# Nine chunks of attention ahead of the first MLP, two token blocks side by side from its first step

## The chip, the cores and the metric

One core of one Trainium2 chip runs the whole program. The metric is the device time of one execution in microseconds (us). The engines are TensorE (PE in the profile, its weight loads PEld), VectorE (DVE), ScalarE (ACT) and GpSimd (POOL); all DMAs are issued from SyncE's queue (SP).

## The reference

Three stages follow one another in float32. Attention runs over B=4 batches, H=8 heads, S=768 steps, head size 48; the two MLPs run over the 3072 tokens of 384 features that attention gives.

```python
for t in range(S):
    state = alpha[:, :, t, :, None] * state + einsum('bhd,bhe->bhde', k[:, :, t], v[:, :, t])
    y[:, :, t] = einsum('bhd,bhde->bhe', q[:, :, t], state)
x = y as (3072 tokens, 384)
h = x @ w_in                      # 384 -> 2048
x = (h * sigmoid(h)) @ w_out      # 2048 -> 384
out = (sigmoid(x @ w_gate) * (x @ w_val)) @ w_out2   # 384 -> 1536 -> 384
```

The weights arrive as 64-bit floats and are turned into float32 on the chip.

## The kernel before, in words

**Attention** is cut into 24 chunks c of 128 tokens, six to a batch. For a chunk, `prep(c, step)` (L262) makes cumulative products of alpha by two scans on DVE: G backward (L277) and A forward (L287). The keys are multiplied by G (L285), the queries by A (L290), and AE (L283) is the decay of the state over the chunk. `scores(c)` (L296) transposes the keys (tile T) and multiplies keys with queries into two PSUM banks (tile S, L310). `scores_done(c)` masks S into M on DVE (L323), copies T to KT on ACT (L326) and squares G and A for a range check on ACT (L260). `results(c)` multiplies the state W with the queries (L338), adds M times the values (L345) and multiplies KT with the values (L355): this last product, U, is what the chunk adds to the state. U lies in the first bank of the chunk's own S. `state(c)` adds U to W on DVE (L363, a copy at L365 for the first chunk of a batch) and multiplies W by AE of the next chunk (L367, one instruction of 112x448). The last chunk of a batch has no T and no U, the first no L338. `y_out(c)` copies the result on ACT (L382) and moves it by six small DMAs (L385, L387) into tile xf; `x_out(c)` splits xf into a rounded part xh on ACT (L394) and a rest xl (L396). The products at L283, L285, L290, L367 and L396 run on POOL for chunks up to ALONE=8, later on DVE.

**The first MLP** runs over items (b, f): block b of 512 tokens (four chunks, six blocks), slice f of 128 of the 2048 features. `mm_in` is nine matmuls of 128x512 into a bank of `ps_h` (two banks, tag h), `act` applies Silu (L568) and splits the result into gh (ACT, L576) and gl (DVE, L577), and `mm_out` is nine matmuls (L549 to L551) that add to the block's three output banks. `mm_out` of an item follows two items later. Block 0 holds the banks of group 0, the other blocks those of group 1; `x2_out` empties them after the last slice.

**Weights** are converted by `Way`. A pair j holds one or two weight tiles (pairs 0 to 2 hold one, then w_in's slice j-1 and w_out's slice j-2, 18 pairs). `bit()` does one sixth of a pair: bits 0 to 2 are L459, L461 and L463 on DVE (with L451 on ACT in bit 0), bit 3 is L482 and L486 on ACT, the load of the pair after next and L494 on DVE, bit 4 is L496 and L497 on DVE, bit 5 is L504 on POOL. `half(True)`, `half(False)` do half a pair with the same operations, two pairs interleaved; raw and temporary tiles are used again two pairs later.

**The order** is written by hand; each engine runs its instructions in that order. The front loop (L690 to L702) runs over the LEAD=5 first chunks: scores of c+1, `states()` (that is `state(c-1)`), `prep` of c+2 with `scores_done(c+1)` between its steps, `x_out(c-1)`, results of c, `y_out(c)`, then CONV[c] bits, 21 in all. Then follow seven items of block 0 alone (LAG=7) with two halves each, in which chunks 5 to 8 are done; then nine times an item of block 0 and one of block 1 with one half each; then the rest of block 1, with chunks 9 to 11 at (1, 10) to (1, 14); then blocks 2 to 5, each with four chunks. SCORES and RESULTS say at which item, and at which place in it (0 behind `mm_in`, 1 behind `mm_out`), a chunk's steps stand; `prep` lies three and two items ahead of the scores.

The second MLP has the same form with two products in; its weights are converted in the last block of the first and in its own first steps.

Of the kernel before, what the change touches and what calls it, by code (L numbers as in the profile page):

```python
# [7 lines left out]
F32 = mybir.dt.float32  # L8
# [5 lines left out]
AF = mybir.ActivationFunctionType  # L14
# [3 lines left out]
P = 128  # L18
# [3 lines left out]
C = 128  # L22
# [11 lines left out]
BLOCKS = [(N * i, N) for i in range(NT // N)]  # L34
NB = len(BLOCKS)

LEAD = 5
LAG = 7

ALONE = 8  # L40
WARM = 3

BITS = 6
SINGLE = 3
CONV = {1: 5, 2: 5, 3: 6, 4: 5}

SCORES = {6: (0, 1, 0), 7: (0, 3, 0), 8: (0, 5, 0), 9: (1, 10, 0), 10: (1, 11, 1), 11: (1, 13, 0)}
RESULTS = {5: (0, 0, 0), 6: (0, 2, 0), 7: (0, 4, 0), 8: (0, 6, 0), 9: (1, 11, 0), 10: (1, 12, 1), 11: (1, 14, 0)}
for _c in range(12, NC):
    SCORES[_c] = (_c // 4 - 1, (0, 4, 8, 11)[_c % 4], 0)  # L50
    RESULTS[_c] = (_c // 4 - 1, (2, 6, 10, 13)[_c % 4], 0)

# [125 lines left out]
def gated_attention_then_mlps(ctx: ExitStack, tc: tile.TileContext, qka, a0, v, w_in, w_out, w_gate, w_val, w_out2, out):  # L178
# [83 lines left out]
    def prep(c, step, p0=0, p1=NP, mul=None):  # L262


        mul = mul or (nc.gpsimd if c <= ALONE else nc.vector)
        t = qk[c]
        lo, hi = p0 * C, p1 * C
        if step == 0:
            if p0 == 0:
                Gt[c] = ap.tile([DP, NP * C], F32, tag="G", name="G", bufs=2)  # L270
                At[c] = ap.tile([DP, NP * C], F32, tag="A", name="A", bufs=2)
            g = Gt[c]
            nc.vector.memset(g[:, hi - 1 : hi], 1.0)
            a_next = t[:, A_OFF + hi - 1 : A_OFF + lo : -1]
            d_g = dg[:, NP * C - 2 :: -1] if lo == 0 and hi == NP * C else dg[:, hi - 2 : lo - 1 : -1] if lo else dg[:, hi - 2 :: -1]
            g_r = g[:, hi - 2 : lo - 1 : -1] if lo else g[:, hi - 2 :: -1]
            nc.vector.tensor_tensor_scan(g_r, a_next, d_g, 1.0, op0=ALU.mult, op1=ALU.add)  # L277
            whole = ap.tile([DP, NP], F32, tag="whole", name="whole")
            nc.vector.tensor_scalar(whole[:, p0:p1], g[:, lo:hi:C], LEAST, None, op0=ALU.max)
            nc.vector.reciprocal(d1[:, lo:hi:C], whole[:, p0:p1])  # L280
            if c % CB:
                AE[c] = ap.tile([DP, NP], F32, tag="aend", name="aend", bufs=2)
                mul.tensor_tensor(AE[c], a0s[:, c, :], g[:, 0::C], op=ALU.mult)  # L283
            k = t[:, NP * C + lo : NP * C + hi]
            mul.tensor_tensor(k, k, g[:, lo:hi], op=ALU.mult)  # L285
        elif step == 1:
            nc.vector.tensor_tensor_scan(At[c][:, lo:hi], t[:, A_OFF + lo : A_OFF + hi], d1[:, lo:hi], 0.0, op0=ALU.mult, op1=ALU.add)  # L287
        else:
            q = t[:, lo:hi]
            mul.tensor_tensor(q, q, At[c][:, lo:hi], op=ALU.mult)  # L290
# [39 lines left out]
    def results(c, g):  # L330


        y = Y[c] = bank(g)
        first = c % CB == 0
        if not first:
            for p in range(NP):

                nc.tensor.matmul(  # L338
                    y[:DP, p * C : (p + 1) * C], W[:, p], qk[c][:, p * C : (p + 1) * C], start=p == 0, stop=False, skip_group_check=True
                )  # L340
        for p in range(NP):
            m = M[c, p // 2]
            for j in range(2):
                r = 64 * j
                nc.tensor.matmul(  # L345
                    y[r : r + D, p * C : (p + 1) * C], vt[c][:, 2 * p + j], m[:, j, p % 2], start=first and p == 0, stop=True, skip_group_check=True
                )
        s = S.pop(c)
        if not last_of(c):
            U[c] = s[:DP, 0, : NP * DP].rearrange("r (p d) -> r p d", p=NP)  # L350
            kt = KT.pop(c)
            for p in range(NP):
                for j in range(2):
                    r = 64 * j
                    nc.tensor.matmul(U[c][r : r + D, p, r : r + D], kt[:, p, r : r + D], vt[c][:, 2 * p + j], start=True, stop=True)  # L355

    def state(c):

        u = U.pop(c)
        for r in (0, 64):  # L360
            s, x = W[r : r + D, :, r : r + D], u[r : r + D, :, r : r + D]
            if c % CB:
                nc.vector.tensor_tensor(s, x, s, op=ALU.add)  # L363
            else:
                nc.vector.tensor_copy(s, x)  # L365
        mul = nc.gpsimd if c <= ALONE else nc.vector
        mul.tensor_tensor(W, W, AE[c + 1].rearrange("r (p d) -> r p d", d=1).to_broadcast([DP, NP, DP]), op=ALU.mult)  # L367

    def block_of(c):
        for b, (t0, n) in enumerate(BLOCKS):  # L370
# [18 lines left out]
    def x_out(c):  # L389
        b, o = block_of(c)  # L390
        if o == 0:
            xh[b], xl[b] = (X(i, F32R) for i in x_at[b])
        x = xf.pop(c)
        nc.scalar.activation(xh[b][:, :, o : o + C], x, AF.Copy, accum_out=chk[:, c, 2:3])  # L394
        mul = nc.gpsimd if c <= ALONE else nc.vector
        mul.tensor_tensor(xl[b][:, :, o : o + C], x, xh[b].bitcast(F32)[:, :, o : o + C], op=ALU.subtract)  # L396


# [240 lines left out]
    with tc.manual_schedule():  # L639
# [28 lines left out]
        def states():  # L668
            while late and (last_of(late[0]) or late[0] + 1 in AE):
                c = late.pop(0)  # L670
                if not last_of(c):
                    state(c)

        def results_done(c):
            late.append(c)
            if c >= LEAD:
                states()
            y_out(c)
            if c + 4 < NC:
                load_chunk(c + 4)  # L680
                load_values(c + 4)
# [6 lines left out]
            prep(1, s)  # L688
        scores_done(0)
        for c in range(LEAD):  # L690
            scores(c + 1, (c + 1) % 2, True)
            states()
            prep(c + 2, 0)
            scores_done(c + 1)
            prep(c + 2, 1)
            prep(c + 2, 2)
            if c:
                x_out(c - 1)
            results(c, c % 2)
            results_done(c)  # L700
            for _ in range(CONV.get(c, 0)):
                way1.bit()  # L702
        states()
        way1.n_half = 2 * SINGLE

        def steps(items):

            at = {x: i for i, x in enumerate(items)}
            todo = {}

            def put(i, place, what, c):
                todo.setdefault((i, place), []).append((what, c))

            for c, (b, f, end) in SCORES.items():
                put(at[b, f], end, "scores", c)
                if c > LEAD + 1:
                    put(at[b, f] - 3 if c != ALONE + 1 else at[0, LAG - 2], 2, "prep0", c)
                    put(at[b, f] - 2, 2, "prep1", c)
            for c, (b, f, end) in RESULTS.items():
                put(at[b, f], end, "results", c)  # L720
                put(at[b, f] + 1 if c != ALONE else at[1, NF1 - LAG - 1], 1, "x_out", c)
            put(0, 1, "x_out", LEAD - 1)
            return todo

        items = [(0, f) for f in range(LAG)]
        for f in range(LAG, NF1):
            items += [(0, f), (1, f - LAG)]
        items += [(1, f) for f in range(NF1 - LAG, NF1)] + [(b, f) for b in range(2, NB) for f in range(NF1)]
        todo = steps(items)

        def tensor(i, place):
            for what, c in todo.get((i, place), ()):
                g = int(c <= ALONE)
                if what == "scores":
                    scores(c, g, False)
                elif what == "results":
                    results(c, g)

        def others(i, place):
            for what, c in todo.get((i, place), ()):  # L740
# [13 lines left out]
        for i, (b, f) in enumerate(items):  # L754
            if (b, f) == (NB - 1, 0):
                at_stack.close()
                bp["b"] = main.enter_context(tc.tile_pool(name="bp", bufs=3))
                bp["x"] = main.enter_context(tc.tile_pool(name="bx", bufs=NX))
                way2.load(0)
                way2.n_half = -2  # L760
            h = mm_in(ps_h, "h", "in", b, f)
            tensor(i, 0)
            way = way1 if i < 2 * NF1 - LAG else way2 if b == NB - 1 else None
            act(b, f, h, None, "out", way)
            others(i, 0)
            others(i, 2)
            if len(pend) > 2:
                mm_out()
            tensor(i, 1)
            others(i, 1)  # L770
            if i < LAG:
                way1.half(True)
                way1.half(False)
            if (b, f) == (NB - 1, NF1 - 4):
                x2_split(0)
            if (b, f) == (NB - 1, NF1 - 1):
                x2_split(1)
# [66 lines left out]
```

## Time and profile before

| | us |
|---|---|
| median of 3 runs (1008.43 to 1008.48) | 1008.44 |
| profiled execution | 1007.8 |
| its span, first to last instruction | 1006.1 |
| PE busy | 957.5 (95%) |
| DVE busy | 521.8 (52%) |
| ACT busy | 385.7 (38%) |
| POOL busy | 127.1 (13%) |

The span is cut into stages by what PE does: the front loop to about 59 us, block 0 alone and the catching up to about 140 us, and from there to 997 us a PE that hardly waits. A busy DVE includes time in which one of its instructions stands blocked, so durations of one kind of instruction are compared with the shortest of that kind.

### The profile page before, as it was taken

Reading aid. Unit: us, or ns where it says so; the run is one execution under the profiler, and the core shown is the slowest. Engines: PE = TensorE matmul, PEld = TensorE weight load, DVE = VectorE, ACT = ScalarE, POOL = GpSimd, SP = SyncE. Lnnn points to the kernel's source line nnn. Section 1 sums busy time; section 2 is a strip of 40 time slices with the busy share of each in tenths; the row PEclk is TensorE's granted clock in tenths of the full one; section 3 lists DMA queues with packets and bytes.
Section 4 is the critical chain, followed back from the end, with each engine's and each line's share of the span. In section 5 each row is a group of like instructions: output and inputs, shape, how many; then the busy total and the mean of one; then the engine's idle time right before and its main releaser. Section 6 shows DMA issues by size and latency. Waiting matters only on the chain.

```text
span 1006.1 us, 12880 instructions
## 1 busy us (share of the span) xinstructions
PE 957.5 (95%) x5008; PEld 786.3 (78%) x5008; DVE 521.8 (52%) x782; ACT 385.7 (38%) x713; POOL 127.1 (13%) x117
## 2 busy tenths in 40 slices
PE   6577899999999999999999999999999999999996
PEld 4465678877888888888888888888888888888885
DVE  8999888464554454453589755663222222222221
ACT  3344566444433433443457443343222222221221
POOL 4554433200000000000033122220000000000000
PEclk8778899999999999999999999999999999999999
DMA  7665352012112112000322111100100000000001
GB/s 184 174 164 160 107 165 83 0 45 87 44 51 80 44 44 78 18 8 13 130 95 94 63 64 64 63 0 1 63 1 1 32 1 0 32 1 1 32 1 35
DMA packets 40038, 58.38 MB, mean 58 GB/s; under 512 B 5216, under 2 KB 28928, under 8 KB 39968
## 3 DMA queue, kind: packets, MB, share of 16 engines
q1 hardware_dynamic: 39968, 57.47, 19.4%
q8 instruction: 41, 0.67, 0.3%
q14 instruction: 29, 0.24, 0.1%
HBM read 48.02 MB, written 4.72 MB: 52 GB/s over the span
## 4 chain that ended last, share of the span: by engine, by line
PE 85%; DVE 9%; issue 2%; POOL 1%; ACT 1%; DMA 1%; SPq 0%; DVEq 0%; POOLq 0%; ACTq 0%
PE h L549 12%; PE h L551 12%; PE h L550 12%; PE s L549 8%; PE s L551 7%; PE s L550 7%; PE y L551 4%; PE y L549 4%; PE y L550 4%; PE v L549 3%; PE v L551 3%; PE v L550 3%; PE s L310 2%; PE y L345 2%; PE y L338 2%
## 5 line engine op out<-in xcount | busy, mean ns | idle before, releaser
L549 PE MATMUL h<-x,w 128*128 128x512 f32 x582 | 228.5, 393 | 4.1 <-ACT w L486 2.3
L551 PE MATMUL h<-x,w 128*128 128x512 f32 x582 | 227.7, 391 | 1.5 <-POOL w L504 1.5
L577 DVE TENSOR_TENSOR gl<-g,gh 128x512 fp32r<-128x512 f32 x168 | 130.0, 774 | 190.8 <-ACT gh L576 190.8
L550 PE MATMUL h<-x,w 128*128 128x512 f32 x582 | 227.5, 391 | 0.0
L576 ACT ACTIVATE gh<-g 128x512 fp32r<-128x512 f32 x168 | 106.2, 632 | 157.9 <-DVE g L571 154.9
L549 PE MATMUL s<-gl,w 128*128 128x512 f32 x336 | 135.8, 404 | 1.5 <-DVE gl L577 1.5
L549 PEld LDWEIGHTS h<-x,w 128*128 128x128 f32 x582 | 109.8, 189 | 29.6 <-ACT w L486 3.5
L550 PE MATMUL s<-gh,w 128*128 128x512 f32 x336 | 132.0, 393 | 0.0
L551 PE MATMUL s<-gh,w 128*128 128x512 f32 x336 | 132.0, 393 | 0.0
L551 PEld LDWEIGHTS h<-x,w 128*128 128x128 f32 x582 | 109.6, 188 | 26.0 <-POOL w L504 2.8
L568 ACT ACTIVATE g<-h 128x512 f32<-128x512 f32 x96 | 57.2, 596 | 184.2 <-PE h L551 184.2
L550 PEld LDWEIGHTS h<-x,w 128*128 128x128 f32 x582 | 109.6, 188 | 23.0
L571 DVE TENSOR_TENSOR g<-v,g 128x512 f32<-128x512 f32 x46 | 31.8, 692 | 178.7 <-PE v L551 178.7
L504 POOL TENSOR_TENSOR w<-tmp,w 128x384 fp32r<-128x384 f32 x36 | 44.3, 1251 | 443.7 <-ACT w L486 443.7
L570 ACT ACTIVATE g<-h 128x512 f32<-128x512 f32 x72 | 43.1, 599 | 144.4 <-PE h L551 144.4
L549 PEld LDWEIGHTS s<-gl,w 128*128 128x128 f32 x336 | 63.5, 189 | 17.5 <-DVE gl L577 1.9
L551 PEld LDWEIGHTS s<-gh,w 128*128 128x128 f32 x336 | 63.7, 189 | 13.8
L550 PEld LDWEIGHTS s<-gh,w 128*128 128x128 f32 x336 | 63.7, 190 | 12.3
L550 PE MATMUL y<-gh,w 128*128 128x512 f32 x168 | 66.0, 393 | 0.0
L549 PE MATMUL y<-gl,w 128*128 128x512 f32 x168 | 65.9, 393 | 0.0
L551 PE MATMUL y<-gh,w 128*128 128x512 f32 x168 | 65.8, 391 | 0.0
L551 PE MATMUL v<-x,w 128*128 128x512 f32 x138 | 53.8, 390 | 0.0
(114 smaller groups left out, 1170.9 us busy)
## 6 DMA issues: line engine op xcount, KB each, us to landing
x<-in_moe_w_out SPq DMA_DIRECT2D x16, 384.0 KB, 4.4
x<-in_qka SPq DMA_DIRECT2D x12, 448.0 KB, 4.3
qk<-in_qka SPq DMA_DIRECT2D x11, 448.0 KB, 4.3
v<-in_v SPq DMA_DIRECT2D x24, 192.0 KB, 4.2
x<-in_moe_w_in SPq DMA_DIRECT2D x16, 288.0 KB, 3.7
raw<-in_moe_w_gate SPq DMA_DIRECT2D x12, 384.0 KB, 3.6
raw<-in_moe_w_val SPq DMA_DIRECT2D x12, 384.0 KB, 3.9
raw<-in_moe_w_out SPq DMA_DIRECT2D x12, 384.0 KB, 3.8
```

The source lines that it names most:

```text
L310: nc.tensor.matmul(S[c][:, j, p * C : (p + 1) * C], t[r : r + D, NP * C + p * C : NP * C + (p + 1) * C], t[r : r + D, p * C : (p + 1) * C] ...
L338: nc.tensor.matmul(y[:DP, p * C : (p + 1) * C], W[:, p], qk[c][:, p * C : (p + 1) * C], start=p == 0, stop=False, skip_group_check=True)
L345: nc.tensor.matmul(y[r : r + D, p * C : (p + 1) * C], vt[c][:, 2 * p + j], m[:, j, p % 2], start=first and p == 0, stop=True, skip_group_c ...
L504: nc.gpsimd.tensor_tensor(l, b[:, i * SW : (i + 1) * SW].bitcast(F32), h.bitcast(F32), op=ALU.subtract)
L549: nc.tensor.matmul(ps, wh, x_l, start=first, stop=False)
L550: nc.tensor.matmul(ps, wh, x_h, start=False, stop=False)
L551: nc.tensor.matmul(ps, wl, x_h, start=False, stop=last)
L568: nc.scalar.activation(g, h, AF.Silu)
L570: nc.scalar.activation(g, h, AF.Sigmoid)
L571: nc.vector.tensor_tensor(g, val, g, op=ALU.mult)
L576: nc.scalar.activation(gh, g, AF.Copy)
L577: nc.vector.tensor_tensor(gl, g, gh.bitcast(F32), op=ALU.subtract)
```

## The change

LEAD becomes 9: the front loop does chunks 0 to 8, and `prep` of c+2 stands as a whole ahead of `scores_done(c+1)`, with `states()` of chunk 8 right behind its results. CONV spreads the same 21 bits as three to each of the chunks 2 to 8. From the first item on, blocks 0 and 1 alternate; at the six slices in SKIP block 0 goes ahead alone, so that it ends at item 25 of 0 to 31. Each of the first 28 items has one half of a pair, the five in MORE a second one. Chunks 9, 10 and 11 stand at (1, 12) to (1, 15), and one more `mm_out` is done ahead of block 2. In the front loop U is put into a bank of `ps_h` and no longer into S. The keys' product (L285) and AE (L283) go from POOL to DVE for chunks 1 to 8, and the decay of W (L367) goes from one POOL instruction to four ACT instructions of 112x112, each with a scale per partition, for states 0 to 7, and to DVE for state 8.

```diff
-LEAD = 5
-LAG = 7
-ALONE = 8
+LEAD = 9
+SKIP = (3, 6, 9, 12, 14, 15)
-CONV = {1: 5, 2: 5, 3: 6, 4: 5}
-SCORES = {6: (0, 1, 0), 7: (0, 3, 0), 8: (0, 5, 0), 9: (1, 10, 0), 10: (1, 11, 1), 11: (1, 13, 0)}
-RESULTS = {5: (0, 0, 0), 6: (0, 2, 0), 7: (0, 4, 0), 8: (0, 6, 0), 9: (1, 11, 0), 10: (1, 12, 1), 11: (1, 14, 0)}
+CONV = {2: 3, 3: 3, 4: 3, 5: 3, 6: 3, 7: 3, 8: 3}
+MORE = (4, 8, 12, 16, 20)
+SCORES = {9: (1, 12, 0), 10: (1, 13, 1), 11: (1, 14, 1), 12: (2, 0, 0)}
+RESULTS = {9: (1, 13, 0), 10: (1, 14, 0), 11: (1, 15, 0), 12: (2, 2, 0)}
+X_OUT = {8: (1, 11), 11: (1, 15)}
+DECAYS = {10: ((1, 9), (1, 10)), 11: ((1, 13), (1, 13)), 12: ((1, 14), (1, 15))}
...
     def prep(c, step, p0=0, p1=NP, mul=None):
-        mul = mul or (nc.gpsimd if c <= ALONE else nc.vector)
+        mul = mul or (nc.gpsimd if c < LEAD else nc.vector)
...
-                mul.tensor_tensor(AE[c], a0s[:, c, :], g[:, 0::C], op=ALU.mult)
+                nc.vector.tensor_tensor(AE[c], a0s[:, c, :], g[:, 0::C], op=ALU.mult)
             k = t[:, NP * C + lo : NP * C + hi]
-            mul.tensor_tensor(k, k, g[:, lo:hi], op=ALU.mult)
+            nc.vector.tensor_tensor(k, k, g[:, lo:hi], op=ALU.mult)
...
-            U[c] = s[:DP, 0, : NP * DP].rearrange("r (p d) -> r p d", p=NP)
+            u = ps_h.tile([P, N], F32, tag="h", name="u")[:DP] if c < LEAD else s[:DP, 0]
+            U[c] = u[:, : NP * DP].rearrange("r (p d) -> r p d", p=NP)
...
-        mul = nc.gpsimd if c <= ALONE else nc.vector
-        mul.tensor_tensor(W, W, AE[c + 1].rearrange("r (p d) -> r p d", d=1).to_broadcast([DP, NP, DP]), op=ALU.mult)
+        if c < LEAD - 1:
+            for p in range(NP):
+                nc.scalar.activation(W[:, p], W[:, p], AF.Copy, scale=AE[c + 1][:, p : p + 1])
+        else:
+            nc.vector.tensor_tensor(W, W, AE[c + 1].rearrange("r (p d) -> r p d", d=1).to_broadcast([DP, NP, DP]), op=ALU.mult)
...
         for c in range(LEAD):
-            scores(c + 1, (c + 1) % 2, True)
+            if c + 1 < LEAD:
+                scores(c + 1, (c + 1) % 2, True)
             states()
-            prep(c + 2, 0)
-            scores_done(c + 1)
-            prep(c + 2, 1)
-            prep(c + 2, 2)
+            if c + 2 <= LEAD:
+                for s in range(3):
+                    prep(c + 2, s)
+            if c + 1 < LEAD:
+                scores_done(c + 1)
...
-        items = [(0, f) for f in range(LAG)]
-        for f in range(LAG, NF1):
-            items += [(0, f), (1, f - LAG)]
-        items += [(1, f) for f in range(NF1 - LAG, NF1)] + [(b, f) for b in range(2, NB) for f in range(NF1)]
+        items, f1 = [], 0
+        for f in range(NF1):
+            items.append((0, f))
+            if f not in SKIP:
+                items.append((1, f1))
+                f1 += 1
+        mixed = len(items) + 2
+        items += [(1, f) for f in range(f1, NF1)] + [(b, f) for b in range(2, NB) for f in range(NF1)]
...
-            way = way1 if i < 2 * NF1 - LAG else way2 if b == NB - 1 else None
+            way = way1 if i < mixed else way2 if b == NB - 1 else None
...
-            if i < LAG:
+            if i in MORE:
                 way1.half(True)
                 way1.half(False)
+            if (b, f) == (1, NF1 - 1):
+                mm_out()
```

## Rows read from the trace of the kernel before

**Rows 1.** The page's slices: busy tenths and granted clock, 40 equal slices of the span.

```profile
DVE  8999888464554454453589755663222222222221
PEclk8778899999999999999999999999999999999999
```

**Rows 2.** Timeline of DVE, front chunk 3: start, duration (us), line, operation, idle before.

```profile
39.62 0.71 DVE L363 TENSOR_TENSOR state<-s,state 48x192 f32<-48x192 f32 x2
...
40.48 2.00 DVE L277 TENSOR_TENSOR_SCAN G<-qk,dg 112x511 f32<-112x511 f32 x1
...
42.94 1.29 DVE L323 TENSOR_TENSOR m<-s,causal 128x512 f32<-128x512 f32 x2
44.14 1.22 DVE L287 TENSOR_TENSOR_SCAN A<-qk,d 112x512 f32<-112x512 f32 x1
...
45.71 1.44 DVE L497 TENSOR_TENSOR x<-x 128x384 f32<-128x384 f32 x1
47.07 2.10 DVE L459 TENSOR_SCALAR x<-x 128x384 uint32<-128x384 uint32 x1
...
50.74 0.72 DVE L363 TENSOR_TENSOR state<-s,state 48x192 f32<-48x192 f32 x2
```

**Rows 3.** Timeline of POOL over the same stretch.

```profile
40.48 0.93 POOL L367 TENSOR_TENSOR state<-state,aend 112x448 f32<-112x448 f32 x1 [1.00 <-DVE G L273]
...
42.78 1.27 POOL L285 TENSOR_TENSOR qk<-qk,G 112x512 f32<-112x512 f32 x1
45.44 1.30 POOL L290 TENSOR_TENSOR qk<-qk,A 112x512 f32<-112x512 f32 x1 [1.38 <-DVE A L287]
46.69 1.31 POOL L396 TENSOR_TENSOR x<-xf,x 128x384 fp32r<-128x384 f32 x1
47.97 0.99 POOL L504 TENSOR_TENSOR w<-x,w 128x384 fp32r<-128x384 f32 x1
```

**Rows 4.** Timeline of DVE: the first state, a free L497, chunk 9's L285.

```profile
19.17 0.72 DVE L365 COPY state<-s 48x192 f32<-48x192 f32 x2 [0.16 <-PE s L355]
...
29.34 0.56 DVE L497 TENSOR_TENSOR x<-x 128x384 f32<-128x384 f32 x1
...
120.10 0.68 DVE L285 TENSOR_TENSOR qk<-qk,G 112x512 f32<-112x512 f32 x1
```

**Rows 5.** Groups by line and shape, 0 to 75 us: count, busy us, mean ns.

```profile
L486 ACT ACTIVATE w<-x 128x384 fp32r<-128x384 f32 x5 | 2.5, 511 | 0.8 <-DVE x L497 0.8
...
L260 ACT ACTIVATION_READ_ACCUMULATOR G<-G 112x1 f32 x6 | 1.2, 192 | 0.0
```

**Rows 6.** Timeline of PE: end of the front loop.

```profile
53.72 2.05 PE L338 MATMUL y<-qk,state 112*112 112x128 f32 x8
...
59.19 0.50 PE L549 MATMUL h<-x,w 128*128 128x512 f32 x1 [1.29 <-POOL x L396]
```

**Rows 7.** Timeline of DVE: L459, which begins a pair, twice in succession.

```profile
154.59 0.57 DVE L459 TENSOR_SCALAR x<-x 128x768 uint32<-128x768 uint32 x1 [0.92 <-POOL w L504]
...
161.75 0.56 DVE L459 TENSOR_SCALAR x<-x 128x768 uint32<-128x768 uint32 x1 [0.91 <-POOL w L504]
```

**Rows 8.** Timeline of PE, 205 to 251 us: chunks 9 to 11, entry of block 2.

```profile
207.73 1.16 PE L310 MATMUL s<-qk 48*128 48x128 f32 x16 [2.04 <-ACT x L600]
...
213.05 1.04 PE L338 MATMUL y<-qk,state 112*112 112x128 f32 x8
...
219.14 0.50 PE L549 MATMUL h<-x,w 128*128 128x512 f32 x1
...
234.24 1.08 PE L345 MATMUL y<-m,v 128*48 128x128 f32 x16
...
242.31 0.47 PE L549 MATMUL h<-x,w 128*128 128x512 f32 x1 [0.60 <-DVE x L396]
...
250.26 0.39 PE L549 MATMUL s<-gl,w 128*128 128x512 f32 x1
250.94 0.39 PE L549 MATMUL s<-gl,w 128*128 128x512 f32 x1
```

More of the change, by code (lines that the diff above doesn't have):

```diff
@@ L44 @@
 SINGLE = 3
-CONV = {1: 5, 2: 5, 3: 6, 4: 5}
-SCORES = {6: (0, 1, 0), 7: (0, 3, 0), 8: (0, 5, 0), 9: (1, 10, 0), 10: (1, 11, 1), 11: (1, 13, 0)}
-RESULTS = {5: (0, 0, 0), 6: (0, 2, 0), 7: (0, 4, 0), 8: (0, 6, 0), 9: (1, 11, 0), 10: (1, 12, 1), 11: (1, 14, 0)}
-for _c in range(12, NC):
+CONV = {2: 3, 3: 3, 4: 3, 5: 3, 6: 3, 7: 3, 8: 3}
[4 more added lines that the diff above has]
+DECAYS = {10: ((1, 9), (1, 10)), 11: ((1, 13), (1, 13)), 12: ((1, 14), (1, 15))}
+for _c in range(13, NC):
     SCORES[_c] = (_c // 4 - 1, (0, 4, 8, 11)[_c % 4], 0)
@@ L394, in x_out @@
         nc.scalar.activation(xh[b][:, :, o : o + C], x, AF.Copy, accum_out=chk[:, c, 2:3])
-        mul = nc.gpsimd if c <= ALONE else nc.vector
+        mul = nc.gpsimd if c < LEAD else nc.vector
         mul.tensor_tensor(xl[b][:, :, o : o + C], x, xh[b].bitcast(F32)[:, :, o : o + C], op=ALU.subtract)
@@ L675, in results_done @@
             late.append(c)
-            if c >= LEAD:
+            if c >= LEAD - 1:
                 states()
@@ L702, in gated_attention_then_mlps @@
                 way1.bit()
-        states()
         way1.n_half = 2 * SINGLE
@@ L715, in steps @@
                 put(at[b, f], end, "scores", c)
-                if c > LEAD + 1:
-                    put(at[b, f] - 3 if c != ALONE + 1 else at[0, LAG - 2], 2, "prep0", c)
-                    put(at[b, f] - 2, 2, "prep1", c)
+                if c > LEAD:
+                    first, then = (at[x] for x in DECAYS[c]) if c in DECAYS else (at[b, f] - 3, at[b, f] - 2)
+                    put(first, 2, "prep0", c)
+                    put(then, 2, "prep1", c)
             for c, (b, f, end) in RESULTS.items():
                 put(at[b, f], end, "results", c)
-                put(at[b, f] + 1 if c != ALONE else at[1, NF1 - LAG - 1], 1, "x_out", c)
-            put(0, 1, "x_out", LEAD - 1)
-            return todo
-        items = [(0, f) for f in range(LAG)]
-        for f in range(LAG, NF1):
-            items += [(0, f), (1, f - LAG)]
-        items += [(1, f) for f in range(NF1 - LAG, NF1)] + [(b, f) for b in range(2, NB) for f in range(NF1)]
+                put(at[X_OUT[c]] if c in X_OUT else at[b, f] + 1, 1, "x_out", c)
+            put(at[X_OUT[LEAD - 1]], 1, "x_out", LEAD - 1)
+            return todo
+        items, f1 = [], 0
[6 more added lines that the diff above has]
+        items += [(1, f) for f in range(f1, NF1)] + [(b, f) for b in range(2, NB) for f in range(NF1)]
         todo = steps(items)
@@ L732, in tensor @@
             for what, c in todo.get((i, place), ()):
-                g = int(c <= ALONE)
                 if what == "scores":
-                    scores(c, g, False)
+                    scores(c, 0, False)
                 elif what == "results":
-                    results(c, g)
+                    results(c, 0)
         def others(i, place):
```

## The prediction

> **What bounds the kernel now.** I read the slices of the page first [rows 1]: the granted clock is at 0.7 to 0.8 and DVE at 8 or 9 tenths in the first seven or so slices, and from about 140 us on PE runs at its full clock with hardly a gap. There three matmuls of 128x512 take 0.68 us [rows 8], 0.2267 each, and a chunk of attention about 4.1: from its first state product (213.05) to the first matmul behind the next chunk's scores (219.14) are 6.09 us, of which one `mm_out` is 2.04 [rows 8]. So every microsecond that PE loses is lost ahead of 140 us or in a short wait, and I price the change by one point: the first matmul of block 2, at 242.31 [rows 8]. From there on both programs do the same, but that the new one has nine matmuls (2.04 us) fewer left.
>
> Between PE's first MLP matmul, 59.19 [rows 6], and 242.31 lie 183.1 us. PE's work there is 558 matmuls (126.5) and some 6.5 chunks less what the last and first of a batch leave out (24): 150.5. So 32.6 us are lost, 2.0 and 0.6 of them in the waits of 207.73 and 242.31 [rows 8], the rest where block 0 alone has a pair of weights converted per 4 us of matmuls.
>
> The front loop itself is the timeline of DVE [rows 2] beside that of POOL [rows 3]. Chunk 3 takes 50.74 - 39.62 = 11.12 us, and DVE always has something. Three of its instructions are stretched, each until a POOL instruction ends: the G scan by 0.93, the length of POOL's L367 beside it; L497 takes 1.44 where a free one takes 0.56 [rows 4], behind L290; L459 takes 2.10, waiting out L396 and L504. That is some 3.6 us, and DVE's own work is 7.5. The mask L323, which reads PSUM, lies beside POOL's L285 and isn't stretched (two in 1.29).
>
> **The change: a front chunk.** DVE's own instructions: state 0.8, G 1.1, the small ones between G and the next big one 0.55 (with AE), keys 0.65 (0.68 for one on DVE [rows 4]), A 1.15, masks 1.2: 5.5 us [rows 2, 4]. Three bits of a single pair are three instructions of about 0.5 each (0.56 for the free L497 [rows 4]): 7.0. POOL keeps L290 (1.30), L396 (1.31) and L504 every second chunk (0.99) [rows 3]. L290 now starts when A ends and so lies beside the masks: hidden, but for 0.1; L396 falls upon the bits and blocks them by its 1.3; L504 comes at a chunk's end, half of it beside the state addition, 0.1 to 0.2 per chunk. Sum 8.5 us per chunk. Bounds: 7.0, nothing blocked, and 10.1, all 3.1 us of POOL blocking.
>
> The keys' move is the edit with the least in it. On POOL they lay under the masks at no cost to DVE [rows 2, 3]; on DVE they cost 0.65, and give the place under the masks to L290, which had cost 0.88: a gain of 0.2. The Trainium skill (Perfetto Trace Analysis, Optimizing Scalar/DVE Operations) says that GpSimd and DVE share a read port, so that moving work between them might not help; by that alone the move would gain nothing, the chunk would be 8.7 and the sum 1.2 us longer. The rows side with it nearly.
>
> The decay's move takes L367's 0.93 off POOL, and with it the stretch of G. On ACT it is four instructions of 112 elements. The trace has none with a scale per partition; the nearest are 0.192 for one element and 0.511 for 384 [rows 5], so four take 0.8 to 2.0; I take 1.05, near the short one. It is covered in chunks 2 to 7: the matmuls that wait for it stand behind the next scores on PE, which U's own bank now lets start without waiting for the state (it lay in the scores' banks before). Queued behind it on ACT are KT and the squares, which nobody needs soon. Without cover, in chunks 1 and 8, it is on the path. The Trainium skill (ScalarE: Activation LUTs, What ACT_TABLE_LOAD costs) puts such an ACTIVATE at 186 ns and 0.833 ns per element, with 93 more for a scale that is a pointer, and its rules leave multiplication to VectorE; estimated from that page four are 1.2 us, which would make the sum 0.3 longer.
>
> The front in time: the first state addition is at 19.17 [rows 4]; A of chunk 1 no longer waits for the keys on POOL, so 18.7. Chunk 1 has no bits: at least DVE's 5.5, at most twice PE's 4.1 (PE is at the lower of its two levels, 1.2 GHz, here: L338 takes 2.05 at 53.72 [rows 6] and 1.04 at 213.05 [rows 8]); I take 7.4. Six chunks of 8.5 follow: 77.1. Chunk 8 has nothing left for DVE but the state: 0.75, the decay 1.05, then L338 to U at the lower level, 59.19 - 1.29 - 53.72 = 4.2 [rows 6]. The first MLP matmul is at **83.1** (bounds on the chunk: 74 to 93).
>
> **The change: two blocks side by side.** Items 0 to 31 and the nine matmuls put ahead: 567 matmuls, 128.5 us, and chunks 9 to 11, 3 x 4.1 less 1.0 for what chunk 11 leaves out: 11.3. On top of that:
> - *Clock*: PE comes out of the front at the lower level; the first nine matmuls take up to 2.0 longer, and some of the next: 2.8 (0 to 4).
> - *Conversion*: an undisturbed pair with two items takes 161.75 - 154.59 = 7.17 us, bound by DVE, ACT and POOL in turn (L459 waits for L504) [rows 7]. Here 15 pairs go with 25 items, 1.67 items per pair, so 0.2 less: 7.0, or 3.5 per half; PE needs 4.08 per item. DVE starts late by the state, its decay and the three bits of chunk 8 (twice as wide: 2.3). Put down item by item, its gl comes behind by 2.5 us at item 21, the first after the fifth item of MORE, and by no more than 1.5 earlier. `mm_out` waits for it: 3.0 (0 to 8; the halves would have to take 3.7 for 8).
> - *Block 0's banks*: as at 207.73, 2.0.
> - *Block 2's last x*: chunk 11's results lie behind the last `mm_in`; from the end of L345 (234.24 + 1.08) to block 2's matmul were 7.0 us [rows 8], through ACT, six DMAs, ACT and DVE. Two `mm_out` (4.1) cover it where before there was one `mm_in` more: 2.7 (0.6 before).
> - 0.5 for chunks that follow each other more closely.
>
> Sum of the waits 11.0; of the stretch 128.5 + 11.3 + 11.0 = 150.8. Block 2 starts at 83.1 + 150.8 = 233.9, instead of 242.31, with 2.04 less to do: the span is 1006.1 - 8.4 - 2.0 = 995.7. Of the profiled execution (1007.8) 1.7 lie around the span, and the median is 0.6 above it: **998.0**.
>
> So of the 32.6 us lost so far 21.6 are won, 24 us of front are added and 12.5 of attention leave the stretch.
>
> **Rivals.**
> 1. *POOL still blocks all it does* (slower). The place is the front, the mechanism the lock seen in [rows 2, 3]: L290 and L396 come back to back, DVE's bit waits out both, as L459 waited out two, and L504 falls on G. At 10.1 per chunk the front ends at 92.7 and the median is 1007.6; from 10.24 on the kernel is slower, and at 10.6, half way to the 11.12 of now, it is 1010.6. Against it: L323 isn't stretched, and three of POOL's five products lie on other engines.
> 2. *The conversion can't keep up* (no change). If a half costs 3.7 and PE, waiting, falls to its lower level for some items, as in [rows 1] below 140 us, 6 to 9 us are lost: 1004 to 1008.
> 3. *DVE's own work alone counts* (faster still). L396 finds ACT's and PSUM's gaps, the chunk is 7.7 and the lag nothing: 83.1 - 4.8, waits 8: 990.
> 4. *The front is PE's*, not DVE's: at the lower level a chunk takes 8.1 of PE, and with a wait for the decay 9: 1001. Then DVE would have gaps.
>
> **How the numbers follow.** Forecast 998, with rival 4 near it: 0.50; rival 3: 0.19; rival 2: 0.14; rival 1: 0.17. The range takes in the chunk's bounds from 7.6 to 10.1 and the lag's: 988 to 1009. A measurement of this kernel tells 0.2% (2 us) from no change. Faster by more than that: all of the forecast and rival 3, a fifth of rival 2: 0.72. Within it: most of rival 2 and a part of 1: 0.13. Slower: the rest of rival 1 with what hasn't been thought of: 0.15.
>
> **What would show it.** In the profile of the changed kernel: state additions on DVE 8.5 us apart from chunk 2 on; G at about 1.1; L323 beside L290; PE's first MLP matmul at 83; after it no PE wait of more than about 3, on gl, and one of about 2.7 on `xl` at block 2, at 234. Rival 1 shows as L459 or L461 of 2 us and more, rival 2 as PE waits on L486, L504 or gl and a clock below full after 100 us. The prediction is wrong if the loads of the next chunks (issued behind six small DMAs of `y_out`) come later than G: then DVE waits for a DMA.

## The result, and the profile after

| | kernel before | changed kernel |
|---|---|---|
| median (lowest to highest), us | 1008.46 (1008.43 to 1011.1) | 993.43 (992.1 to 994.42) |
| profiled execution, us (its span) | 1007.8 (1006.1) | 993.17 (991.4) |
| first MLP matmul of PE, us | 59.19 | 78.32 |
| first matmul of block 2, us | 242.31 | 228.46 |
| from there to the end, us | 763.8 | 762.9 |

The ratio of the times is 0.9844 (95% interval 0.9824 to 0.9864): 1.56% faster. The forecast was 998.0, its range 988 to 1009. In the profiled execution the span was predicted at 995.7 and is 991.4. The two points by which the sum was made say where the 4.3 us are: the front ended 4.8 us earlier than predicted (78.32 for 83.1), the stretch up to block 2 was right to 0.7 us (150.14 for 150.8), and the rest of the program took 1.2 us more than I had carried over (762.9 for 761.8). Where the time is won is between the two points: of the 32.6 us that PE lost there in the kernel before, 10.3 are left (150.14 less 139.8 for PE's work), and some 13 us of attention are no longer there, for 19.1 us of longer front.

The first view is the page's slices, which answer to [rows 1]. DVE is as busy as before in the first seven slices but for the fourth (6 for 9), in which it waits for chunk 8's results and then for weights; the granted clock is at 0.9 or more from the fourth slice on, before from the sixth.

```profile
DVE  8896888664445444452788666653222222232221
...
PEclk7769999999999999999999999999999999999999
```

The next is the timeline of DVE over the chunk that answers to [rows 2] (start, duration, line, operation; lines moved by four to eight: L277 is now L281, L285 L289, L287 L291, L323 L327, L363 L368, L459 L467, L461 L469). From state addition to state addition are 49.73 - 41.77 = 7.96 us, where the kernel before took 11.12.

```profile
41.77 0.72 DVE L368 TENSOR_TENSOR state<-u,state 48x192 f32<-48x192 f32 x2
...
42.64 1.36 DVE L281 TENSOR_TENSOR_SCAN G<-x,dg 112x511 f32<-112x511 f32 x1
...
44.34 0.68 DVE L289 TENSOR_TENSOR x<-x,G 112x512 f32<-112x512 f32 x1
44.93 1.22 DVE L291 TENSOR_TENSOR_SCAN A<-x,d 112x512 f32<-112x512 f32 x1
46.18 1.29 DVE L327 TENSOR_TENSOR m<-s,causal 128x512 f32<-128x512 f32 x2
47.38 0.49 DVE L467 TENSOR_SCALAR x<-x 128x384 uint32<-128x384 uint32 x1
47.91 1.24 DVE L469 SCALAR_TENSOR_TENSOR x<-x,x 128x384 uint32<-128x384 uint32 x1
49.25 0.56 DVE L471 SCALAR_TENSOR_TENSOR x<-x 128x384 f32<-128x384 f32 x1
49.73 0.72 DVE L368 TENSOR_TENSOR state<-u,state 48x192 f32<-48x192 f32 x2
```

POOL's timeline over the same stretch has three products left of the five of [rows 3]; L294 (before: L290) begins 0.2 us behind the masks L327 and runs beside them, and L404 (before: L396) falls on the bits.

```profile
41.93 0.99 POOL L512 TENSOR_TENSOR w<-x,w 128x384 fp32r<-128x384 f32 x1 [0.95 <-DVE x L505]
46.38 1.28 POOL L294 TENSOR_TENSOR x<-x,A 112x512 f32<-112x512 f32 x1 [3.45 <-DMA x<-in_qka]
47.61 1.12 POOL L404 TENSOR_TENSOR x<-xf,x 128x384 fp32r<-128x384 f32 x1
```

PE's timeline shows the entry of the MLP, the waits for gl (in brackets: idle time before, and what ended it), the scores of chunk 9, which waited 2.04 in [rows 8] and here wait for nothing, and block 2.

```profile
78.32 0.58 PE L557 MATMUL h<-x,w 128*128 128x512 f32 x1
78.74 0.40 PE L558 MATMUL h<-x,w 128*128 128x512 f32 x1
78.97 0.39 PE L559 MATMUL h<-x,w 128*128 128x512 f32 x1
...
87.00 0.50 PE L557 MATMUL s<-gl,w 128*128 128x512 f32 x1 [2.19 <-DVE gl L585]
...
108.03 0.50 PE L557 MATMUL s<-gl,w 128*128 128x512 f32 x1 [0.33 <-DVE gl L585]
...
125.50 0.50 PE L557 MATMUL s<-gl,w 128*128 128x512 f32 x1 [0.84 <-DVE gl L585]
...
142.78 0.50 PE L557 MATMUL s<-gl,w 128*128 128x512 f32 x1 [0.62 <-DVE gl L585]
...
160.24 0.50 PE L557 MATMUL s<-gl,w 128*128 128x512 f32 x1 [0.82 <-DVE gl L585]
...
197.94 1.16 PE L314 MATMUL s<-qk 48*128 48x128 f32 x16
...
228.46 0.55 PE L557 MATMUL h<-x,w 128*128 128x512 f32 x1 [2.64 <-DVE x L404]
228.81 0.63 PE L558 MATMUL h<-x,w 128*128 128x512 f32 x1
229.24 0.63 PE L559 MATMUL h<-x,w 128*128 128x512 f32 x1
```

What the wait of 2.19 stands behind is seen on DVE: chunk 8's last bit ends at 82.42 (L471, 0.96 us from 81.46), and DVE then waits 2.03 us for the next pair's weights. On SP's queue that load was issued at 77.54, behind six small DMAs of chunk 7's results (L393 and L395, 70.92 to 74.94) and five other loads, two of them for the same pair. The later pairs begin 7.16 us apart where nothing comes between, each when POOL has finished the one before, as in [rows 7]; with the items of MORE the mean of the thirteen from 84.45 to 174.96 is 6.96.

```profile
84.45 0.56 DVE L467 TENSOR_SCALAR x<-x 128x768 uint32<-128x768 uint32 x1 [2.03 <-DMA x<-in_moe_w_out]
...
91.61 0.56 DVE L467 TENSOR_SCALAR x<-x 128x768 uint32<-128x768 uint32 x1 [0.91 <-POOL w L512]
```

### The profile page after: what moved, and what is told of

It reads as the page before. It is cut to its first block, busy times and chain, and to the rows that moved or that the text cites. A ratio compares the mean times of both kernels' runs of the same rounds, so it can differ in the third digit from the quotient of the medians.

```text
span 991.4 us, 12901 instructions
## 1 busy us (share of the span) xinstructions
PE 952.4 (96%) x5008; PEld 783.7 (79%) x5008; DVE 509.2 (51%) x798; ACT 393.4 (40%) x741; POOL 104.6 (11%) x94
## 4 chain that ended last, share of the span: by engine, by line
PE 84%; DVE 7%; POOL 3%; issue 2%; DMA 2%; ACT 2%; SPq 1%; DVEq 0%; ACTq 0%
PE h L557 12%; PE h L558 12%; PE h L559 12%; PE s L557 7%; PE s L558 7%; PE s L559 7%; PE y L558 3%; PE y L559 3%; PE y L557 3%; PE v L557 3%; PE v L558 3%; PE v L559 3%; POOL w L512 2%; PE y L349 2%; PE y L342 2%; PE s L314 2%
## 5 line engine op out<-in xcount | busy, mean ns | idle before, releaser
L585 DVE TENSOR_TENSOR gl<-g,gh 128x512 fp32r<-128x512 f32 x168 | 134.6, 801 | 179.6 <-ACT gh L584 179.6
```

What stands on the lines that cost most here:

```text
L585: nc.vector.tensor_tensor(gl, g, gh.bitcast(F32), op=ALU.subtract)
```

## The experiments

They answer two questions: which part of the change makes the front chunk short (E1 to E5, E10), and what the waits behind the front depend on (E6 to E9, E11). All are compared by their ratio to the kernel before; the changed kernel has 0.9844, 0.001 is 1 us, and the interval of a ratio is about 1.7 us to either side. So a difference of two ratios under some 2.5 us is settled by the trace if at all.

**E1. The decay back on POOL.**

```
-            for p in range(NP):
-                nc.scalar.activation(W[:, p], W[:, p], AF.Copy, scale=AE[c + 1][:, p : p + 1])
+            nc.gpsimd.tensor_tensor(W, W, AE[c + 1]... , op=ALU.mult)
```

> The changed kernel with one thing undone: the decay of the state W goes back to one instruction on POOL for the states of the front loop. Theory (the POOL instruction beside the G scan stretches the scan by its own length, as in the kernel before, where G took 2.00 us with 0.93 of POOL beside it): the front chunks are 0.9 us longer where a G scan follows a state addition, that is after states 0 to 4 and 6, one of them absorbed by the wait for chunk 4's load; PE's first MLP matmul moves from 78.3 to about 83 and the time from 993.4 to about 998. Rival (the decay's latency ahead of L342 on PE bounds the chunk, whatever engine does it): no change, 993 to 994, and G stays at 1.2.

Ratio 0.9867 (0.985 to 0.9883), 2.3 us more; the first MLP matmul comes at 84.38, 6.1 later, of which part comes back since the first gl is then waited for 1.21 us only. The interaction is another one than in [rows 2, 3]: there G was stretched to 2.00 by the decay beside it. Here G is free (1.37) and the decay itself takes 1.85 where it took 0.93, waiting G out; behind G it then holds up a DVE instruction of 112x4, L283, for 0.72 us where it takes 0.17 otherwise. DVE's timeline, then POOL's:

```profile
45.78 0.72 DVE L283 TENSOR_SCALAR whole<-G 112x4 f32<-112x4 f32 x1
```

```profile
44.62 1.85 POOL L372 TENSOR_TENSOR state<-state,aend 112x448 f32<-112x448 f32 x1
```

That happens in five chunks, 2.7 us in all, and is less than half of the 6.1. The larger part is the decay's latency, by a way through three engines: PE's L342 waits for POOL's decay (3.55 us at 37.48), ACT's copy of the chunk's result (L387) waits for PE (1.85 us at 41.51), and the conversion's ACT instruction L487 stands behind that copy in ACT's order. (In chunk 5 ACT's order waits instead for the small DMAs of chunk 4's results, 5.70 us, which leave behind such a late copy.) In the bits of chunks 3, 5 and 7 DVE waits 1.53, 1.99 and 0.82 us for L487; in the changed kernel these waits are 0.32, 0.18 and nothing. DVE's timeline, chunk 3:

```profile
42.57 0.36 DVE L501 TENSOR_TENSOR x<-x 128x384 bf16<-128x384 bf16 x1 [1.53 <-ACT x L487]
```

So the rival, that the decay's latency bounds the chunk, is right in part, though not by PE itself. In the front the move is worth 6.1 us; in the time it is 2.3, which the ratios by themselves don't tell from nothing.

**E2. The keys' product and AE back on POOL.**

```
-                nc.vector.tensor_tensor(AE[c], a0s[:, c, :], g[:, 0::C], op=ALU.mult)
+                mul.tensor_tensor(AE[c], a0s[:, c, :], g[:, 0::C], op=ALU.mult)
-            nc.vector.tensor_tensor(k, k, g[:, lo:hi], op=ALU.mult)
+            mul.tensor_tensor(k, k, g[:, lo:hi], op=ALU.mult)
```

> The changed kernel with one thing undone: the keys' product and AE go back to POOL for chunks 1 to 8. In the changed order A follows on the keys' product, so the 1.27 us on POOL no longer lie under the masks but beside the A scan. Theory: A is stretched by about 1.2, DVE saves 0.65: 0.6 us per chunk, 4 to 5 in all, 998. The prediction's own figure (a gain of 0.2 per chunk by the move) would give 995. Rival (DVE isn't what bounds a chunk): 993 or a little faster, as DVE has 0.65 less to do.

Ratio 0.9843 (0.9825 to 0.986): no difference, and not the 998 expected. In the new order the keys on POOL lie beside A, not beside the masks, and A takes 2.03 instead of 1.22; DVE's 0.68 for the keys and A's 0.81 cancel. DVE's timeline:

```profile
45.84 2.03 DVE L291 TENSOR_TENSOR_SCAN A<-x,d 112x512 f32<-112x512 f32 x1
```

This chunk takes 8.15 us for the 7.96 above, others with the keys on POOL 0.3 more than in the changed kernel, and the first MLP matmul comes 2.15 later (80.47). But the wait of 2.19 for the first gl is gone, so the time shows none of it: there the front had only run ahead of the weights.

**E3. The state sums back in the scores' bank.**

```
-            u = ps_h.tile([P, N], F32, tag="h", name="u")[:DP] if c < LEAD else s[:DP, 0]
-            U[c] = u[:, : NP * DP].rearrange("r (p d) -> r p d", p=NP)
+            U[c] = s[:DP, 0, : NP * DP].rearrange("r (p d) -> r p d", p=NP)
```

> The changed kernel with one thing undone: U goes back into the first bank of the chunk's scores, so that the scores of c+1 wait for the state addition of c-1. Theory: PE then goes state 0.75, scores 2.08, L342 to L360 4.85 at the lower clock level, 7.7 with its handoffs about 8.0, as long as DVE's 7.7: 1 to 3 us in the front, 995 to 996. Rival (DVE alone bounds the chunk, the bank is worth nothing): 993 to 994. Other rival (the bank is the main gain, PE bounds the chunk): over 1 us per chunk, above 1000.

Ratio 0.9882 (0.9863 to 0.99), 3.8 us more, twice what I expected. PE's scores now wait for the state addition, which the trace names by the DVE instruction behind it:

```profile
43.87 1.16 PE L314 MATMUL s<-qk 48*128 48x128 f32 x16 [2.43 <-DVE G L277]
```

The first MLP matmul is 2.85 later. On DVE it comes by the same way as in E1: PE's results, ACT's copy and the conversion's L489 behind it, for which DVE waits 0.88, 1.54 and 1.02 in the bits of chunks 3, 5 and 7 (DVE's timeline, chunk 5):

```profile
58.42 0.36 DVE L503 TENSOR_TENSOR x<-x 128x384 bf16<-128x384 bf16 x1 [1.54 <-ACT x L489]
```

So the bank, which the forecast had counted only as the cover of the decay, has a price of its own. Whether it is dearer than the decay's move (3.8 and 2.3 us in the time, 2.85 and 6.1 in the front) the measurement doesn't tell.

**E4. All three undone: the order alone.** The edits of E1 to E3 together.

> The changed kernel with all three moves undone (decay and keys on POOL, U in the scores' banks): the new order of chunks and items alone. Theory, if the three add up: 4.7 + 4.5 + 2 = 11 us more than 993.4, 1004.6, so that the order alone is worth 4 of the 15 us. Rival (the order is the gain, the moves are small): below 997. Rival (the order alone is a loss): above 1008.5.

Ratio 0.9899 (0.9883 to 0.9916): 1.0% faster than before, where 1004.6 was expected. The order of the work (nine chunks ahead, blocks 0 and 1 together from the first item) carries 10 of the 15.7 us by itself. How that divides between the chunks ahead, the two blocks side by side, the masks' place and the `mm_out` ahead of block 2 wasn't run. Its front ends only at 85.92, later than the 83.1 of the forecast.

**E5. The three moves alone, in the kernel before.** The same three edits, made in the old kernel with its five chunks in front; state 8's decay goes to ACT here too.

> The kernel before with the three moves alone (keys' product and AE on DVE, the decay of states 0 to 8 as four ACT instructions, U of the front chunks in the h banks), in its own order of chunks and items. Theory: the four front chunks with 5 to 6 bits lose G's stretch (0.9) and a part of the others, some 1 to 1.5 us each, and the stage of block 0 alone, where DVE and POOL are full, 0.5 to 1 for each of its chunks: 6 to 8 us less than 1008.4, about 1001. Rival (the moves only pay in a long front): 1006 to 1008.

Ratio 0.9992 (0.9983 to 1.0002): nothing. I had expected 1001. DVE's timeline over the chunk of [rows 2]:

```profile
39.47 0.71 DVE L364 TENSOR_TENSOR state<-u,state 48x192 f32<-48x192 f32 x2
...
40.33 1.23 DVE L277 TENSOR_TENSOR_SCAN G<-qk,dg 112x511 f32<-112x511 f32 x1
...
41.94 0.68 DVE L285 TENSOR_TENSOR qk<-qk,G 112x512 f32<-112x512 f32 x1
...
45.34 1.64 DVE L501 TENSOR_TENSOR x<-x 128x384 f32<-128x384 f32 x1
46.91 2.10 DVE L463 TENSOR_SCALAR x<-x 128x384 uint32<-128x384 uint32 x1
...
50.57 0.71 DVE L364 TENSOR_TENSOR state<-u,state 48x192 f32<-48x192 f32 x2
```

A chunk takes 11.10, before 11.12. G is free now (1.23 for 2.00), but DVE has the keys (0.68) in exchange, and L501 and L463 wait out POOL's products just as before. In the old order the masks come between the keys and A, so the product that follows A falls upon the bits, whichever engine has the keys. That the masks' place alone would free the moves in this kernel wasn't run; a front of five chunks, the rival, is a second difference.

**E10. The changed kernel with the masks back between the keys and A.**

```
-                for s in range(3):
-                    prep(c + 2, s)
+                prep(c + 2, 0)
             if c + 1 < LEAD:
                 scores_done(c + 1)
+            if c + 2 <= LEAD:
+                prep(c + 2, 1)
+                prep(c + 2, 2)
```

> The changed kernel with the masks of c+1 back between the first and the other steps of prep of c+2, as in the kernel before. Theory (the moves of keys and decay pay because, with the masks behind the A scan, the queries' product on POOL lies beside the masks, which it doesn't stretch; this is why the moves alone gave nothing in the old order): that product then lies beside the bits, each chunk with bits is 1.0 to 1.3 us longer, 6 to 8 us in the front, 999 to 1001, and L469, L502 or L505 stretch as L459 and L497 did before. Rival (the order is indifferent, the moves didn't pay in the old order for another reason): 993 to 995.

Ratio 0.987 (0.9853 to 0.9887), 2.6 us more: less than expected, in the direction expected, and hardly more than the ratios tell apart; the trace is plainer. The first MLP matmul comes 4.6 later (82.93), and a chunk takes 52.15 - 43.34 = 8.81. The difference to 7.96 is in two rows of DVE, L469 (1.24 in the changed kernel) and L471 (0.56), less 0.15 that L467 is shorter:

```profile
43.34 0.71 DVE L368 TENSOR_TENSOR state<-u,state 48x192 f32<-48x192 f32 x2
...
49.32 1.64 DVE L469 SCALAR_TENSOR_TENSOR x<-x,x 128x384 uint32<-128x384 uint32 x1
51.06 1.17 DVE L471 SCALAR_TENSOR_TENSOR x<-x 128x384 f32<-128x384 f32 x1
52.15 0.71 DVE L368 TENSOR_TENSOR state<-u,state 48x192 f32<-48x192 f32 x2
```

With the masks last, POOL's q product (1.28) runs beside an instruction that isn't held up by it. That bears out the reading of E5: between the keys and A the masks cover nothing. What the three moves would bring with the new order of the chunks and the masks in their old place wasn't run.

**E7. The bits a chunk earlier**, so that the double-wide ones of chunk 8 leave its end.

```
-CONV = {2: 3, 3: 3, 4: 3, 5: 3, 6: 3, 7: 3, 8: 3}
+CONV = {1: 3, 2: 3, 3: 3, 4: 3, 5: 3, 6: 3, 7: 3}
```

> The changed kernel with the conversion's bits one chunk earlier (three each for chunks 1 to 7 instead of 2 to 8). Theory: the load of pair 4, which now lands at 84.4, comes a chunk earlier, DVE's wait of 2.03 us for it goes, DVE has 2.4 us less to do behind chunk 8's state, and PE's wait of 2.19 for the first gl goes with the small ones behind it; the bits in chunk 1 take 1.5 us, most of it where DVE waits 1.39 for chunk 4's load: 2 to 4 us less, 989.5 to 991.5. Rival (the bits only move, the front gets longer by what the start of the items wins): 993 to 994.

Ratio 0.9873 (0.9856 to 0.9891): 2.9 us more, where a gain was expected. Chunk 1 now has bits and takes 27.23 - 19.21 = 8.0 where it took 5.4 (1.17 of it DVE waits for ACT's L459); the wait for chunk 4's load is gone, but the first MLP matmul still comes at 80.93, 2.6 later. The first wait for gl is gone, the second grows from 0.33 to 1.33.

**E8. Chunk 10's preparation one item later.**

```
-DECAYS = {10: ((1, 9), (1, 10)), 11: ...
+DECAYS = {10: ((1, 10), (1, 11)), 11: ...
```

> The changed kernel with chunk 10's prep one block-1 item later, at (1, 10) and (1, 11), where the rule of the kernel before would have put it. Theory: DVE is then busy with it when block 0's output banks are to be emptied, and PE waits some 2 us ahead of chunk 9's scores, as it did in the kernel before (2.04 at 207.73): 995 to 995.5. Rival (that wait had another reason): 993 to 994.

Ratio 0.9845 (0.9832 to 0.9859): no difference. Chunk 9's scores wait 0.81 us for ACT's last copy out of block 0's banks, not the 2 us that the forecast had carried over. Where the 2.04 of [rows 8] came from is in DVE's timeline of the kernel before: the end of chunk 9's preparation and the whole of chunk 10's, one behind the other, ahead of the copy L602 that empties a bank and that ACT's last copy waits for. In the changed kernel chunk 9's preparation is done in the front.

```profile
199.07 1.22 DVE L287 TENSOR_TENSOR_SCAN A<-qk,d 112x512 f32<-112x512 f32 x1
...
204.38 1.22 DVE L287 TENSOR_TENSOR_SCAN A<-x,d 112x512 f32<-112x512 f32 x1
...
206.35 0.69 DVE L602 COPY x<-s 128x512 f32<-128x512 f32 x1
```

**E9. The bits of a chunk ahead of its state addition.**

```
             results(c, c % 2)
-            results_done(c)
             for _ in range(CONV.get(c, 0)):
                 way1.bit()
+            results_done(c)
```

> The changed kernel with the conversion's bits of each front chunk ahead of results_done (so ahead of ACT's copy L390, of the y_out DMAs and the next loads on SP, and in chunk 8 ahead of the state addition that DVE waits 5.2 us for). Theory (the first items lose time because pair 4's load lands at 84.4 and chunk 8's bits stand behind the state): the load goes out some 7 us earlier, the bits fall into DVE's wait, PE's 2.19 us wait for the first gl goes and the later ones (0.33, 0.84, 0.62, 0.82) shrink: 3 to 4.5 us less than 993.4, 989 to 990.5. Rival (the waits for gl are the rate of the conversion, not its start): the first wait goes, the later ones grow by as much: 992.5 to 993.5.

Ratio 0.9835 (0.982 to 0.9851): 0.9 us less, which the measurement doesn't tell from nothing. The wait for the first gl is gone, but the pair after that waits longer for its load, and the next gl 1.30 instead of 0.33. DVE's timeline:

```profile
91.99 0.56 DVE L467 TENSOR_SCALAR x<-x 128x768 uint32<-128x768 uint32 x1 [3.72 <-DMA x<-in_moe_w_out]
```

So by these rows an earlier start of the conversion wins nothing while the loads and the rate behind it stay as they are.

**E6. One more `mm_out` ahead of block 2**, to cover the wait of 2.64.

```
             if (b, f) == (1, NF1 - 1):
                 mm_out()
+                mm_out()
```

> The changed kernel with one more mm_out at item (1, 15), so that three instead of two lie between chunk 11's results and block 2. Theory: the wait of 2.64 us for xl at block 2 shrinks by the 2.04 us of these nine matmuls, and the nine matmuls behind it, which ran at the lower level of the clock (0.43 us apart instead of 0.23), run at the upper one: 2.0 + 1.9 = 3 to 4 us less, 989.5 to 990.5. Rival (the clock falls for another reason): 991.4, and the matmuls behind the wait are still 0.43 apart. Rival (gl of the last item of block 1 comes too late for the third mm_out): 992 to 993.4.

Ratio 0.9811 (0.9798 to 0.9825), 3.3 us less than the changed kernel: 990.13 in the median, the lowest of all. The wait shrinks to 1.20, by 1.44 and not by the 2.04 of the matmuls put in; and the matmuls behind it are 0.23 apart, not 0.43 (PE's timeline):

```profile
229.80 0.47 PE L557 MATMUL h<-x,w 128*128 128x512 f32 x1 [1.20 <-DVE x L404]
230.11 0.40 PE L558 MATMUL h<-x,w 128*128 128x512 f32 x1
230.34 0.39 PE L559 MATMUL h<-x,w 128*128 128x512 f32 x1
```

**E11. E6 and E9 together.**

> Both late edits together: the bits ahead of results_done, and one more mm_out ahead of block 2 (alone 990.13). They lie at different places (78 to 175 us and 225 us), so the gains should add: 3.3 for the mm_out and what the bits give alone: 985.5 to 987.5 if that is 3 to 4.5, 989.5 if it is nothing.

Ratio 0.9817 (0.98 to 0.9833), as E6 alone. The order of the bits adds nothing.

## Why the prediction held, and where it didn't

The mechanism was right in the main: the front's length is DVE's, POOL's products stretch it only where they lie beside instructions that they hold up, and what the stretch behind the front loses is small. What it lacked is ACT: E1 and E3 show that a late result on PE reaches DVE through ACT's order. The terms, one by one:

- **A front chunk: 8.5 predicted, 7.7 measured without a wait for DMA.** DVE's own work was right: chunk 1, without bits, takes 24.82 - 19.40 = 5.42 for the 5.5 of the sum. Then come six chunks from 24.82 to 72.55, 47.7 us; the first has 1.39 in it in which DVE waits for chunk 4's load, and the other five take 7.5 to 8.0. That load was issued at 24.07, behind the six small DMAs of chunk 0's results (19.31 to 23.96): the case that the prediction's last sentence named as its refutation, and that the sum left out. It came once, and the shorter chunks more than covered it. The mis-sized term is L404 (1.3, all of it): it is 1.12 long, L467 runs beside part of it, and L469 takes 1.24 instead of 0.56, so 0.7 of it counts. In chunks 3 and 5 it is L504 that is held up, 0.76 and 0.89 instead of 0.36. 5.4 + 1.5 for the bits + 0.7 is 7.6, the lower part of the bounds given (7.0 to 10.1). Six chunks with the wait: -3.3 us.

```profile
27.05 1.22 DVE L281 TENSOR_TENSOR_SCAN G<-qk,dg 112x511 f32<-112x511 f32 x1 [1.39 <-DMA qk<-in_qka]
```

- **Chunk 1: 7.4 predicted, 5.42 measured.** I had set it between DVE's 5.5 and twice PE's 4.1; DVE alone decides. -2.0 us. Its start (19.40 for 18.7) and chunk 8 (5.77 for 6.0) add 0.5 together.
- **The decay on ACT: 1.05 predicted, 1.22 measured** (the row below: 28 of them, 377 ns in the mean; four, overlapping, take 1.21 to 1.23). The estimate by the Trainium skill (ScalarE: Activation LUTs, What ACT_TABLE_LOAD costs) of 1.2 was the better one, and the trace agrees with that page. PE does wait for it, 10.3 us over six chunks, so the next scores alone don't cover it as I had it; DVE, which sets the pace, doesn't. E1 shows that the move shortens the front.

```profile
L373 ACT ACTIVATE state<-state,aend 112x112 f32<-112x112 f32 x28 | 8.6, 377 | 11.9 <-DVE state L368 8.7 <-DVE state L370 3.2
```

- **The keys' move: 0.2 per chunk predicted, 0.2 to 0.3 in E2's chunks, nothing in its time.** The size was right for another reason than mine: on POOL the keys stretch A by 0.81, a little more than the 0.68 that they cost on DVE. The Trainium skill's remark (Perfetto Trace Analysis, Optimizing Scalar/DVE Operations) that moving work between DVE and GpSimd might not help agrees with the time, not with the front (2.15 us).
- **The clock at the entry: 2.8 predicted, 0.2 measured.** Only the first matmul, 78.32, took longer (0.42 to the next); from 78.74 on they are 0.23 apart. In the other profiles of the new order it is 0.1 to 0.9 (E3). I had taken the mean of a slice of [rows 1] for a stretch of matmuls, and read seven slices below 0.9 where there are five. The kernel before had the answer in PE's timeline, in rows that I didn't take: behind 59.19 its matmuls follow at the full clock as well.

```profile
59.53 0.39 PE L550 MATMUL h<-x,w 128*128 128x512 f32 x1
59.76 0.40 PE L551 MATMUL h<-x,w 128*128 128x512 f32 x1
```

- **The waits for gl: 3.0 predicted, 4.8 measured.** The part by rate was right in its sum: pairs come 6.96 apart in the mean for the 7.0 of the forecast, and the four waits behind the first sum to 0.33 + 0.84 + 0.62 + 0.82 = 2.6. Not in its places: they come some 17.4 us apart, each for the gl of the item behind one of the first four of MORE, and behind the fifth, where I had put 2.5, the profile names none; the pair begun there is the last, with one tile. The first wait, 2.19, is another load behind six small DMAs, of weights, which the sum left out too.
- **Block 0's banks: 2.0 predicted, none measured.** I had carried a wait over without asking what DVE did ahead of it; E8 has the cause.
- **Block 2's x: 2.7 predicted, 2.64 measured.** Right, and unforeseen is what it does: the matmuls behind it run 0.43 apart and nine take 3.7 us, 228.46 to 232.18, where the same took 2.14 at the full clock in E10. These 1.6 us account for the 1.2 that the rest of the program took above the sum.
- What is left of the stretch is 2.9 us where 0.5 was foreseen. In PE's timeline twenty matmuls stand 0.33 to 0.42 ahead of the next, not 0.23: the first of the stretch, those on either side of each wait, and those behind each piece of attention (87.00 and 87.34). They come to 2.7.

So the stretch of 150.1 was right by luck, by errors that cancel: 2.8 and 2.0 too much, 1.8 and 2.4 too little. Two slips of the prediction changed nothing: 161.75 - 154.59 is 7.16, and of POOL's five products in [rows 3] two, not three, went to other engines.

Of the rivals, the first (POOL blocks all) falls: no L467 or L469 above 1.24 in the front. The second (the conversion can't keep up) is there as a wait of 2.6 in all, and the clock is full from 80 us to block 2. The fourth (the front is PE's) falls, but not by much: in the six chunks DVE has no gap that PE ends, only 0.5 us in which it waits for ACT behind PE's results. The third, DVE's own work alone with 7.7 per chunk, had the chunk as measured and the front to 0.1 us (78.3), the latter by luck: 2.0 too much for chunk 1, against a later start and the wait for chunk 4's load. Nor is its reason borne out, since L404 does hold up the bits. Its 990 is 3.4 short, 2.3 of them in the stretch, where it had no wait for gl, and 1.2 behind block 2's wait. The measured 993.4 lies between it and the forecast, a little nearer to it.

What is won with the whole change comes in the main from the order (E4, 10 us), the rest from the moves that make its front short; the moves in the old order bring nothing (E5). In the new order the single undoings cost 2.3, 0 and 3.8 us, each give or take 2.6, and all together 5.5.

## What to carry to other kernels

Where two engines hold each other up, the order on the one decides as much as the division between them: look for an instruction that its neighbour doesn't stretch (here the masks, which read PSUM, 1.29 with POOL or without), and put the neighbour's longest work beside it, before moving work to another engine. An engine that never waits for PE can still be late by it, through a third whose instructions stand in one order: here the conversion's on ACT, behind the copy of a chunk's result. Carry a wait over to a changed kernel only with its cause: ask what the releasing engine did just ahead of it, and whether that moves. A clock's share in a slice is no price of a matmul; read the distance of the matmuls in the stretch itself.

## What the runs showed of the hardware

A wait of some us in an otherwise full stretch can cost more than itself. The windows below (length, busy time and count of PE, PEld, DVE, ACT and POOL, then the granted clock, DMA share, GB/s) are the 5 us around block 2's first matmuls, of the changed kernel and then of E10. Both waited 2.64 us there. In the first the granted clock falls to 0.79 and the matmuls stand 0.43 apart, which is what 512 columns take at the lower level (512 / 1.2 GHz = 0.427 us); in E10, where the window begins within the wait, it stays at full and they stand 0.23 apart (PE's timeline). Over the 5 us from block 2's first matmul on it is 0.66 in the changed kernel and 1.00 in E10.

```profile
230.00:235.00 5.00, 5.00 (x31) 3.89 (x30) 1.33 (x3) 2.59 (x6) 0.00 (x0) 0.79 0.03 9
```

```profile
230.00:235.00 5.00, 3.16 (x21) 2.63 (x23) 0.56 (x1) 1.40 (x4) 0.00 (x0) 1.00 0.60 181
```

```profile
231.84 0.47 PE L557 MATMUL h<-x,w 128*128 128x512 f32 x1 [2.64 <-DVE x L404]
232.15 0.40 PE L558 MATMUL h<-x,w 128*128 128x512 f32 x1
232.38 0.39 PE L559 MATMUL h<-x,w 128*128 128x512 f32 x1
```

Of the profiles with a wait of 2.6 to 3.5 us at that point all but E10's show a granted clock of 0.91 to 0.96 over 225 to 265 us (the changed kernel, E1 to E4, E7 to E9); of those with 0.6 to 1.4 (the kernel before, E5, E6, E11) all show 1.00. So the fall goes with the length of the wait, and E10 shows that the length alone doesn't settle it; what else does is open. It isn't bound to this place: in E6 the wait for the first gl was 2.82 us, and behind it eight matmuls stand 0.43 apart from 88.98 on, where the changed kernel's, behind a wait of 2.19, stand 0.23 apart. How much of E6's 3.3 us is the shorter wait and how much the clock is therefore only bounded by rows: 1.44 the one, up to 1.6 the other.
